# Order of the score matmuls, path of the row maxima, and order of two DMA groups in a fused attention and MLP block

## The chip, the cores and the metric

The kernel runs on one core of a Trainium2 chip. A core has five engines with a queue each: PE (TensorE, matrix products), DVE (VectorE), ACT (ScalarE), POOL (GpSimd) and SP (SyncE, which here only starts DMA transfers). Each engine works through its own queue in order, and semaphores order the queues among each other. Products go to PSUM, a small memory of banks of 512 float32 values per partition; everything else is in SBUF, with 128 partitions, or in HBM. The metric is the time of one execution on the device, in microseconds (us).

## The reference

One transformer-like block on x of 2048 tokens by 640 features, all in float32. A vector c gives six modulation vectors. Then sliding attention with 32 heads of 20 features, in which a token sees itself and the 255 tokens before it, and a channel MLP with 1536 hidden features:

```python
mod = (_silu(c) @ w_mod).reshape(c.shape[0], 6, 1, -1)
h = _layernorm(x) * (1 + ca) + sa
qkv = h @ wqkv
scores = einsum("bhqd,bhkd->bhqk", q, k) * (Dh ** -0.5)
mask = (i - j >= 0) & (i - j < 256)
p = _softmax(where(mask, scores, -1e9))
x = x + ga * ((p @ v) @ wo)
h = _layernorm(x) * (1 + cb) + sb
x = x + gb * (gelu(_layernorm(h) @ w1 + b1) @ w2 + b2)
```

## The kernel before

**Precision.** Most operands are split into a high and a low part in a reduced float32 format (`F32R`), and a product is the sum of high x high, high x low and low x high. A projected q or k thus has three rows per feature, 60 rows for the 20 features of a head.

**Stages.** First a prologue: the modulation, the first LayerNorm and the first projection units. Then the attention stage, a loop over slots `t` that is written out by hand and runs from about 50 to about 610 us of the span. Last the MLP, with the last pieces of attention's output projection mixed in.

**A slot.** The 2048 tokens are worked on in two halves of 1024 (`HALF`), the 32 heads in eight groups of four (`quad`), and the 1024 queries of a half in eight blocks of 128 (`qb`). There are 2 x 8 x 8 = 128 score slots. In slot `t` the loop issues, in this order:

- a *score batch* (`score_batch`, line 549) with two parts. The part `e` has *transposed* scores, keys on partitions, for the head group of `LAG` = 11 slots ago (`e_batch`). The part `s` has *plain* scores, queries on partitions, for the present block (`s_batch`); they are used only to find the maximum of each row.
- on DVE the mask of `e` (`e_mask`), then the sums P x V of `PVLAG` = 2 slots ago on PE (`pv_stage`, tile `o`), and the exponential of `e` on ACT (`e_exp`, tile `pt`) with two triangular selections on POOL
- on DVE the mask of `s` and the maxima of its rows (`s_max`, tile `nm`)
- the stores of q and k rows that were projected in an earlier slot (`rows_out`, line 435, on SP's queue)
- four quarters `h` = 0 to 3 of planned work (`plan`): projection matmuls (`pp`), weight loads (`w_load`, placed at the head of quarter 0), splits of weights, transposes, reads of projected rows back from HBM (`rows_in`, planned in quarter 3, up to `READ` = 7 slots before their use).

In slots whose transposed part is empty (one in eight of the first half), and in the first 11 and the last slots, the batch has one part only. `e` and `s` have one PSUM buffer each, of 4 heads x 384 columns, which is three banks.

**The halves of the array.** q and k of two heads lie at partitions 0 to 63 and 64 to 127, so a score matmul uses one half of the array's rows, and two matmuls on different halves can run at once. Of the four heads of a buffer, two belong to either half. The four heads lie at 384 columns each, so the middle bank is shared between the halves. `score_batch` sorts the matmuls of a part into six groups: `a`, `b`, `c` on the first half (`a` in the shared bank), `d`, `e`, `f` on the second (`f` in the shared bank). It puts a wait in PE's queue ahead of `f`, until the last matmul of `a` is complete. The order in which the groups are issued stands in two lists: `ONE` for batches with one part and `BOTH` for batches with two, where "0" is the transposed part, if there is one, and "1" the plain part.

**The maxima.** When the eight blocks of a head group are done, their 4 x 8 maxima per partition are negated and split into a high and a low part on DVE (`m_split`, at the end of every eighth slot, into tile `mh`). In the next slot, quarter 1, `m_rows` transposes `mh` on PE, copies the result to SBUF on ACT (tile `mt`), and starts two DMA transfers from ACT's queue, which lay the two parts into rows 60, 61 and 124, 125 of the group's q buffer. The transposed scores of that group then subtract the maximum inside the product, against rows of ones in the k buffer. They start three slots later.

`Ordered` (line 108) passes each instruction on in program order, so line 124, its helper, is the line that nearly all instructions show; they are told apart by their tiles.

Of the kernel before, what the change touches and what calls it, by code (L numbers as in the profile page):

```python
# [9 lines left out]
F32 = mybir.dt.float32  # L10
F32R = mybir.dt.float32r
U32 = mybir.dt.uint32
AF = mybir.ActivationFunctionType
ALU = mybir.AluOpType
# [3 lines left out]
P = 128  # L18
# [5 lines left out]
NQB = HALF // P  # L24
QUADS = H // 4
# [3 lines left out]
NSLOT = 4  # L29
# [24 lines left out]
X_COST = 1.7  # L54

ONE = "0a 0d 0b 0e 0c 0f".split()
BOTH = "0a 0d 1a 0b 0e 0c 1d 1c 0f 1b 1f 1e".split()

EXTRA = {
# [44 lines left out]
def f32(ap):  # L104
    return ap.bitcast(F32)
# [24 lines left out]
def block_kernel(ctx: ExitStack, tc: tile.TileContext, x, wqkv, wo, w1, b1, w2, b2, c, crow, wmod, wcol, sel, outT):  # L130
    core = tc.nc
    nc = Ordered(tc)
    matmul, transpose = nc.tensor.matmul, nc.tensor.transpose
# [20 lines left out]
    idn = const.tile([P, P], F32, name="idn")  # L154
# [45 lines left out]
    base = ctx.enter_context(tc.tile_pool(name="base", bufs=1, side="left"))  # L200
    prj = prj_ctx.enter_context(tc.tile_pool(name="prj", bufs=1, side="left"))
    att_ctx = ExitStack()
    att = att_ctx.enter_context(tc.tile_pool(name="att", bufs=1, side="right"))
# [13 lines left out]
    def aside(shape, name):  # L217

        kind = "e" if now[0] < LAG - 1 else "o" if now[0] < 2 * NQB * QUADS else "t"
        return pools[kind].tile(shape, F32, tag=kind, name=name)  # L220
# [168 lines left out]
    qb_ = [att.tile([P, 2, HALF], F32R, name=f"qbuf{i}") for i in range(NSLOT)]  # L389
# [45 lines left out]
    def rows_out():  # L435

        due = [w for w in writes if w[-1] < now[0]]
        for half, kind, j, c2, st, _ in due:
            fs, ts = slice(j * P, (j + 1) * P), slice(half * HALF + c2 * CHUNK, half * HALF + (c2 + 1) * CHUNK)
            two = f32(st) if kind == 0 else f32(st[:, 0:1]).to_broadcast([P, 2, CHUNK])  # L440
            nc.sync.dma_start(qk_scr[kind][fs, 0:2, ts], two)
            nc.sync.dma_start(qk_scr[kind][fs, 2, ts], f32(st[:, kind]))
        del writes[: len(due)]
# [105 lines left out]
    def score_batch(batches):  # L549
# [19 lines left out]
        }  # L569
        order = BOTH if len(batches) == 2 else ONE  # L570
        queue = [(int(k in "def"), mm) for n, k in order for mm in kinds.get((int(n), k), ())]
# [33 lines left out]
        nc.vector.copy_predicated(s[:, :, 2 * P : 384], masks["s"].to_broadcast([P, 4, P]), data)  # L605
        nc.vector.tensor_reduce(it["quad"]["nm"][:, :, it["key"][2]], s[:, :, max(c0, P) : 384], AX.X, ALU.max)

    mh = att.tile([P, P], F32R, name="mh")

    mh_parts = mh[:, 0:64].rearrange("p (e l r) -> p e l r", e=2, l=2)  # L610
    nc.vector.memset(f32(mh)[:, 64:P], 0.0)

    def m_split(it):
        nm, hi, lo = it["quad"]["nm"].rearrange("p (e a) q -> p e (a q)", e=2), mh_parts[:, :, 0], mh_parts[:, :, 1]
        nc.vector.tensor_scalar(hi, nm, -1.0, None, ALU.mult)
        nc.vector.scalar_tensor_tensor(lo, nm, -1.0, f32(hi), ALU.mult, ALU.subtract)

    def m_rows(it):
        half, quad, _, _ = it["key"]
        ps = aside([P, P], f"pm{half}_{quad}")  # L620
        transpose(ps, f32(mh), idn)
        mt = att.tile([64, P], F32, tag="mt", name=f"mt{half}_{quad}")
        nc.scalar.copy(mt, ps[0:64])
        for e in range(2):
            to = qb_[(half * QUADS + quad) % NSLOT][64 * e + 60 : 64 * e + 62]
            nc.scalar.dma_start(f32(to), mt[32 * e : 32 * e + 32])


    def e_parts(it):
# [21 lines left out]
    def e_mask(it, e):  # L651
        if it["mask"] == "do":

            nc.vector.copy_predicated(e[:, :, 0:P], masks["d"].to_broadcast([P, 4, P]), e[:, :, 2 * P : 384])
            return
        for col in (0, 2 * P):
            nc.vector.copy_predicated(
                e[:, :, col : col + P], masks[it["mask"]].to_broadcast([P, 4, P]), negc.to_broadcast([P, 4, P])
            )
# [134 lines left out]
    def r_steps(ch):  # L794

        ts, box = slice(ch * CHUNK, (ch + 1) * CHUNK), {}

        def load():
            pool, tag = (att, "mt") if ch < 2 else (base, "acc")
            box["rd"] = pool.tile([P, P if ch < 2 else D], F32, tag=tag, name=f"rd{ch}")[:, 0:P]  # L800
            nc.sync.dma_start(box["rd"], o_scr[:, DH, ts])

        def invert():
            nc.vector.reciprocal(box["rd"], box["rd"])
            nc.sync.dma_start(r_scr[:, ts], box["rd"])

        return load, invert
# [206 lines left out]
    for c2 in range(2):  # L1014
        for kind in range(2):
            acc = ps_0.tile([P, CHUNK], F32, tag=f"a{c2}{kind}", name=f"pp{c2}_{kind}_0")
# [104 lines left out]
    def take_aside(t, go):  # L1121

        t += AFTER.get(taken[0], 0)
        taken[0] += 1
        while t in asides:
            t += 1
        asides.add(t)
        put(t, 1, go)
        return t

    def lay_units(room):
        used, act = collections.Counter(), collections.Counter()
        for t in asides:
            used[t] += 0.5
        t, turns, where = 0, {}, []
        for i, (key, c2) in enumerate(seq):
            fast = i < FAST
            acc = (lambda i=i: pools["o"].tile([P, CHUNK], F32, tag="o", name=f"ppo{i}")) if fast and i % 2 else None
            mms, ev = unit(*key, c2, gp, acc)
            if key[0] and 2 + c2 in turns:  # L1140
                t = max(t, turns[2 + c2] + 1)
            t0, left = t, list(mms)
            pieces = []
            while left:
                have = room * (t + 1 - FAST) - sum(used[j] for j in range(FAST, t + 1))
                n = len(left) if fast else min(len(left), max(LEAST, int(have + 0.5) + EXTRA.get(t, 0)))
                if len(left) - n < 3 and n < MOST:
                    n = len(left)
                pieces.append((t, left[:n]))
                used[t] += n  # L1150
                left = left[n:]
                t += 1
            where.append((i, key, c2, pieces, ev))
            if key[1] == 2:
                used[t] += V_COST
            if not key[0] and not [1 for k, c in seq[i + 1 :] if not k[0] and c == c2]:

                at = max(t, turns[2] + 5) if c2 else t
                for kt in range(KT):
                    used[at + kt] += X_COST  # L1160
                turns[2 + c2] = at + KT + (1 if c2 else 2)
        return t, where, turns

    lo, hi = 4.0, 16.0
    for _ in range(30):
        room = (lo + hi) / 2
        lo, hi = (lo, room) if lay_units(room)[0] <= LAST else (room, hi)
    _, where, turns = lay_units(hi)
# [34 lines left out]
    for half in range(2):  # L1203
# [4 lines left out]
        for quad in range(QUADS):  # L1208
            if half or quad:
                js = range(4 * quad * DH // P, (4 * quad * DH + 4 * DH - 1) // P + 1)  # L1210
                due = 8 * (half * QUADS + quad)
                for c2 in range(2):
                    t = due + 4 * c2 - READ
                    for kind in range(2):
                        t = max([t, due - 8 * NSLOT + LAG + 8] + [over_at.get((kind, j, c2), -9) + 2 for j in js])
# [3 lines left out]
    for n, ((g, at), lo) in enumerate(zip(((2, 0), (4, 1), (3, 2), (5, None)), MODS)):  # L1219
        steps, rows = mod_steps(g, at)  # L1220
        spread(plan, [step(1, f) for f in steps], lo[0], lo[1])
        t = int(lo[1])
        for f in rows:
            t = take_aside(t, f) + 1
    for ch, when in turns.items():
# [7 lines left out]
        t = when  # L1233
        for kt in range(KT):
            t = take_aside(t, lambda gos=turn[3 * kt : 3 * kt + 3]: [go() for _, go in gos]) + 1
# [26 lines left out]
    for t, nm, go in sorted(tail, key=lambda e: e[:1]):  # L1262
        t = t if t < 128 else 128 + (t - 128) / LATE
        if nm not in ("load", "om"):
            t = max(t, TOMID)
# [19 lines left out]
    for t in range(n + LAG + PVLAG + 4):  # L1285
        now[0] = t
        si = s_items[t] if t < n else None
        u = t - LAG
        ei = e_items[u] if 0 <= u < n else None
        if t == n:  # L1290
            sco_ctx.close()
            pools["t"] = ctx.enter_context(
                tc.tile_pool(name="ps_t", bufs=1, space=PSUM, side="left", reuse_waits="tile")
            )
        turn_m = 8 <= t <= n and t % 8 == 0
        batches = []
        if ei and ei["kbs"]:
            batch, e = e_batch(ei)
            batches.append(batch)
        if si:  # L1300
            batch, *got = s_batch(si)
            batches.append(batch)
        score_batch(batches)
        if ei and ei["kbs"]:
            e_mask(ei, e)
        sums = [(*key, pv_stage(*key)) for key in pv_at.get(t, ())]
        if t not in SUMS_LAST:
            for each in sums:
                pv_copy(*each)
        if ei and ei["kbs"]:  # L1310
            e_exp(ei, e)
        if t in SUMS_LAST:
            for each in sums:
                pv_copy(*each)
        if si:
            s_max(si, *got)
            if t % NQB == NQB - 1:
                m_split(si)
        rows_out()
        for h in range(4):  # L1320
            if h == 1 and turn_m:
                m_rows(s_items[t - 1])
            for go in plan.pop((t, h), ()):
                go()
        for key in pv_at.get(t, ()):
            pv_store(*key)
# [20 lines left out]
    for ch in range(nch):  # L1347
        yhi, ylo = ([y[:, kt] for kt in range(KT)] for y in yT[ch % 2])
        ts = slice(ch * CHUNK, (ch + 1) * CHUNK)
        lo, hi = (4, 9) if ch == 0 else (4 * ch + 5, 4 * ch + 9)  # L1350
# [21 lines left out]
        for f in range(FT):  # L1372
# [7 lines left out]
            pool, tag = (ps_out, f"o{KT - 1}") if (ch, f) == (0, 1) else (ps_h, "h")  # L1380
# [68 lines left out]
```

## Time and profile before

| | us |
|---|---|
| median of three runs | 1017.7 |
| the three runs | 1014.81, 1017.7, 1019.65 |
| span of the profiled execution (its own time from first to last instruction) | 1014.6 |
| PE busy in the span | 962.9 (95%) |
| DVE busy | 576.7 (57%) |
| POOL busy | 513.2 (51%) |
| ACT busy | 443.7 (44%) |

The profiled execution's own time is known by its span; what lies around it is not recorded on the page. Matmuls are pipelined and the ends of their records are modelled, so a record is longer than the time that the matmul keeps others away, and a busy PE is not one at its peak. The time between the starts of two matmuls says more than their lengths. Idle time in the list of waits is counted per engine, and PE's weight loads (PEld) are kept apart from its matmuls (PE). A wait is put down to the instruction that came last by the records. An engine that waits costs nothing by that alone: it matters where PE, busy for 95% of the span, stands behind it.

### The profile page before, as it was taken

Reading aid. Unit: us, or ns where it says so; the run is one execution under the profiler, and the core shown is the slowest. Engines: PE = TensorE matmul, PEld = TensorE weight load, DVE = VectorE, ACT = ScalarE, POOL = GpSimd, SP = SyncE. Lnnn points to the kernel's source line nnn. Section 1 sums busy time; section 2 is a strip of 40 time slices with the busy share of each in tenths; the row PEclk is TensorE's granted clock in tenths of the full one; section 3 lists DMA queues with packets and bytes.
Section 4 is the critical chain, followed back from the end, with each engine's and each line's share of the span. In section 5 each row is a group of like instructions: output and inputs, shape, how many; then the busy total and the mean of one; then the engine's idle time right before and its main releaser. Section 6 shows DMA issues by size and latency. Waiting matters only on the chain.

```text
span 1014.6 us, 19923 instructions
## 1 busy us (share of the span) xinstructions
PE 962.9 (95%) x7712; PEld 761.1 (75%) x7712; DVE 576.7 (57%) x943; ACT 443.7 (44%) x773; POOL 513.2 (51%) x702
## 2 busy tenths in 40 slices
PE   7989999998999999999988889999999999999998
PEld 7767677666677777776666667888888888888886
DVE  5554777887777788777778753454433343333112
ACT  3732555565654455455534544434433333333212
POOL 4332646676774456455535754666455445541221
PEclk7899999999999999999978889999999999999999
DMA  8255858656588467945482124244333234124113
GB/s 297 94 199 162 278 173 267 211 157 176 170 265 245 126 202 245 285 107 161 125 245 62 45 77 130 94 153 140 120 112 87 81 117 135 48 70 154 54 40 117
DMA packets 99429, 152.89 MB, mean 151 GB/s; under 512 B 8904, under 2 KB 42312, under 8 KB 99336
## 3 DMA queue, kind: packets, MB, share of 16 engines
q1 hardware_dynamic: 89032, 142.71, 46.1%
q10 hardware_dynamic: 10304, 8.92, 2.9%
q8 instruction: 61, 1.00, 0.4%
q14 instruction: 32, 0.26, 0.1%
HBM read 99.17 MB, written 51.58 MB: 149 GB/s over the span
## 4 chain that ended last, share of the span: by engine, by line
PE 78%; DVE 11%; ACT 4%; DMA 3%; issue 2%; POOL 1%; SPq 0%; ACTq 0%; DVEq 0%; POOLq 0%
PE h L124 16%; PE out L124 16%; PE pp L124 15%; PE wo L124 7%; PE e L124 6%; PE o L124 6%; PE s L124 6%; DVE nm L124 3%; DVE e L124 3%; ACT pt L124 2%; DVE s L124 2%; PE ppo L124 2%; PE psx L124 1%; DMA o_scr<-oT 1%; PE xt L124 1%
## 5 line engine op out<-in xcount | busy, mean ns | idle before, releaser
L124 POOL TENSOR_SCALAR_AFFINE_SELECT pt<-pt 128x512 f32<-128x512 f32 x192 | 130.5, 680 | 137.3 <-ACT pt L124 123.9
L124 DVE TENSOR_REDUCE nm<-s 128x4 f32<-128x1024 f32 (+1 forms) x128 | 152.7, 1193 | 4.4
L124 POOL TENSOR_TENSOR w2lo<-w2r,w2hi 128x640 fp32r<-128x640 f32 x48 | 75.6, 1575 | 151.8 <-ACT w2hi L124 151.4
L124 ACT ACTIVATE pt<-e 128x1024 f32<-128x1024 f32 (+1 forms) x120 | 133.8, 1115 | 38.4 <-DVE e L124 34.0
L124 PE MATMUL e<-qbuf,kbuf 62*128 62x128 f32 (+2 forms) x792 | 120.7, 330 | 21.5 <-ACT pt L124 21.2
L124 PEld LDWEIGHTS e<-qbuf,kbuf 62*128 62x128 f32 x792 | 82.4, 193 | 62.9 <-ACT pt L124 39.2
L124 PE MATMUL pp<-hhi,whi 128*128 128x512 f32 x275 | 120.1, 437 | 3.9 <-ACT hhi L124 1.5
L124 DVE CAST ghi<-g 128x512 fp32r<-128x512 f32 x48 | 26.5, 553 | 166.3 <-ACT g L124 166.2
L124 PE MATMUL s<-kbuf,qbuf 60*128 60x256 f32 (+2 forms) x744 | 111.3, 304 | 9.5 <-DVE nm L124 8.2
L124 PE MATMUL pp<-hlo,whi 128*128 128x512 f32 x275 | 112.3, 408 | 0.6 <-POOL hlo L124 0.6
L124 PEld LDWEIGHTS s<-kbuf,qbuf 60*128 60x128 f32 x744 | 91.3, 189 | 27.7 <-PE e L124 8.7
L124 PE MATMUL pp<-hhi,wlo 128*128 128x512 f32 x275 | 112.0, 407 | 0.0
L124 DVE COPY_PREDICATED e<-mask_t,e 128x512 f32<-128x512 uint32 x96 | 66.6, 694 | 75.4 <-PE s L124 64.2
L124 ACT COPY oT<-o 128x128 f32<-128x128 f32 x128 | 34.0, 266 | 169.7 <-PE o L124 162.3
L124 PE MATMUL o<-pt,vbuf 128*32 128x128 f32 x2688 | 104.5, 287 | 0.7 <-ACT oT L124 0.4
L124 POOL TENSOR_TENSOR wlo<-wraw,whi 128x128 fp32r<-128x128 f32 x185 | 81.3, 470 | 34.2 <-ACT whi L124 31.8
L124 PE MATMUL out<-ghi,w2hi 128*128 128x512 f32 x240 | 96.1, 400 | 0.0
L124 PE MATMUL h<-yhi,w1hi 128*128 128x512 f32 x240 | 95.8, 399 | 0.0
L124 PE MATMUL out<-ghi,w2lo 128*128 128x512 f32 x240 | 93.9, 391 | 0.0
L124 PE MATMUL out<-glo,w2hi 128*128 128x512 f32 x240 | 93.9, 391 | 0.0
L124 PE MATMUL h<-ylo,w1hi 128*128 128x512 f32 x240 | 93.9, 391 | 0.0
L124 PE MATMUL h<-yhi,w1lo 128*128 128x512 f32 x240 | 93.8, 391 | 0.0
(166 smaller groups left out, 1842.1 us busy)
## 6 DMA issues: line engine op xcount, KB each, us to landing
w2r<-in_w SPq DMA_DIRECT2D x48, 320.0 KB
qbuf<-q_scr SPq DMA_DIRECT2D x60, 240.0 KB
wraw<-in_wqkv SPq DMA_DIRECT2D x38, 320.0 KB
kbuf<-k_scr SPq DMA_DIRECT2D x44, 240.0 KB
q_scr<-stage SPq DMA_DIRECT2D x20, 512.0 KB
k_scr<-stage SPq DMA_DIRECT2D x20, 512.0 KB
o_scr<-oT ACTq DMA_DIRECT2D x64, 128.0 KB
wm<-in_wmod SPq DMA_DIRECT2D x20, 320.0 KB
```

Source lines behind the costliest of these rows:

```text
L124: return self.tc.keep_in_program_order(op(*args, **kw))
```

## The change

Three things are changed, all in the attention stage.

1. In a batch with two parts, all groups of the transposed part are issued first, in the order `a d c e b f`, then all groups of the plain part in the same order. Before, the parts were mixed. The wait ahead of `f` stays as it is, once for each part.
2. `m_split` and its tile are gone. `m_rows` transposes the 32 columns of maxima as they are, and then splits: ACT negates into `mt` and rounds that to the high part, POOL subtracts for the low part. The two DMA transfers are issued from SP's queue; one has the high parts (rows 60 and 124), the other the low parts (rows 61 and 125). The reciprocal sums, which shared the buffer `mt`, get a buffer of their own (`rd`).
3. `rows_out` moves from ahead of the four quarters to the head of quarter 1. On SP's queue it now stands behind what quarter 0 issues, the weight loads above all, and ahead of `m_rows`.

```diff
-BOTH = "0a 0d 1a 0b 0e 0c 1d 1c 0f 1b 1f 1e".split()
+BOTH = "0a 0d 0c 0e 0b 0f 1a 1d 1c 1e 1b 1f".split()
...
-    mh = att.tile([P, P], F32R, name="mh")
-
-    mh_parts = mh[:, 0:64].rearrange("p (e l r) -> p e l r", e=2, l=2)
-    nc.vector.memset(f32(mh)[:, 64:P], 0.0)
-
-    def m_split(it):
-        nm, hi, lo = it["quad"]["nm"].rearrange("p (e a) q -> p e (a q)", e=2), mh_parts[:, :, 0], mh_parts[:, :, 1]
-        nc.vector.tensor_scalar(hi, nm, -1.0, None, ALU.mult)
-        nc.vector.scalar_tensor_tensor(lo, nm, -1.0, f32(hi), ALU.mult, ALU.subtract)
-
     def m_rows(it):
         half, quad, _, _ = it["key"]
-        ps = aside([P, P], f"pm{half}_{quad}")
-        transpose(ps, f32(mh), idn)
-        mt = att.tile([64, P], F32, tag="mt", name=f"mt{half}_{quad}")
-        nc.scalar.copy(mt, ps[0:64])
-        for e in range(2):
-            to = qb_[(half * QUADS + quad) % NSLOT][64 * e + 60 : 64 * e + 62]
-            nc.scalar.dma_start(f32(to), mt[32 * e : 32 * e + 32])
+        ps = aside([4 * NQB, P], f"pm{half}_{quad}")
+        transpose(ps, it["quad"]["nm"].rearrange("p h q -> p (h q)"), idn)
+        hi = att.tile([4 * NQB, P], F32R, tag="mhi", name=f"mhi{half}_{quad}")
+        lo = att.tile([4 * NQB, P], F32R, tag="mlo", name=f"mlo{half}_{quad}")
+        full = att.tile([4 * NQB, P], F32, tag="mt", name=f"mt{half}_{quad}")
+        nc.scalar.mul(full, ps, -1.0)
+        nc.scalar.copy(hi, full)
+        nc.gpsimd.tensor_tensor(lo, full, f32(hi), ALU.subtract)
+        for row, part in ((60, hi), (61, lo)):
+            nc.sync.dma_start(f32(qb_[(half * QUADS + quad) % NSLOT][row::64]), f32(part))
...
-            pool, tag = (att, "mt") if ch < 2 else (base, "acc")
+            pool, tag = (att, "rd") if ch < 2 else (base, "acc")
...
-            if t % NQB == NQB - 1:
-                m_split(si)
-        rows_out()
         for h in range(4):
+            if h == 1:
+                rows_out()
             if h == 1 and turn_m:
                 m_rows(s_items[t - 1])
```

## The prediction

> **What bounds the kernel now.** I read the page first: its span, and the chain that ended last.
>
> ```profile
> span 1014.6 us, 19923 instructions
> PE 78%; DVE 11%; ACT 4%; DMA 3%; issue 2%; POOL 1%; SPq 0%; ACTq 0%; DVEq 0%; POOLq 0%
> ```
>
> PE carries 78% of the chain and DVE 11%. The second question is what PE waits for, so the list of waits comes next, longest first.
>
> ```profile
> DVE e L124 <- PE s L124: 81.8, 79, 3.2
> PE e L124 <- ACT pt L124: 21.2, 25, 2.4
> PE s L124 <- DVE nm L124: 8.2, 20, 1.3
> ```
>
> Both of PE's large waits are in the attention stage, and both are loops from one slot to the next: a batch of transposed scores (`e`) waits until the exponential of the slot before has read the one buffer, and a batch of plain scores (`s`) until the maximum of the slot before has been taken. The first row shows a third thing: the mask of `e` on DVE begins when plain scores end, although it needs `e` alone.
>
> All this happens inside the double batches, so I looked at single slots in the timeline. First PE in a slot where nothing is late, then DVE and ACT in the same slot (columns: start, length, engine, operation, tiles, count).
>
> ```profile
> 322.83 0.44 PE L124 MATMUL e<-qbuf,kbuf 62*128 62x256 f32 x2
> 323.05 0.28 PE L124 MATMUL s<-kbuf,qbuf 60*128 60x256 f32 x1
> ...
> 323.17 0.54 PE L124 MATMUL e<-qbuf,kbuf 62*128 62x128 f32 x3
> 323.46 0.43 PE L124 MATMUL s<-kbuf,qbuf 60*128 60x384 f32 x4
> 323.82 0.54 PE L124 MATMUL o<-pt,vbuf 128*32 128x128 f32 x12
> ```
>
> ```profile
> 323.91 0.70 DVE L124 COPY_PREDICATED e<-mask_t,e 128x512 f32<-128x512 uint32 x1 [1.36 <-PE s L124]
> 324.51 0.69 DVE L124 COPY_PREDICATED s<-mask_t,s 128x512 f32<-128x512 uint32 x1
> 325.24 1.23 DVE L124 TENSOR_REDUCE nm<-s 128x4 f32<-128x1024 f32 x1
> ```
>
> The mixed batch of 6 + 6 matmuls takes 0.99 us from its first matmul to the first `o` (322.83 to 323.82): `e` and `s` fill each other's holes. The mask starts at 1.08, and the maxima are done at 3.64.
>
> **Part 1, the order of the batch.** The `e` matmuls of the two row halves of the array share one bank of the buffer. The program lets the second half's part of it ("f") start only when the first half's part ("a") is complete; PE's own queue stands at that wait. There is one such wait for `e` and one for `s`. Slots that have `e` alone show its price, since nothing else fills the hole.
>
> ```profile
> 593.42 0.88 PE L124 MATMUL e<-qbuf,kbuf 62*128 62x256 f32 x6
> 594.24 0.65 PE L124 MATMUL o<-pt,vcar 128*32 128x128 f32 x16
> 593.42 0.41 PEld L124 LDWEIGHTS e<-qbuf,kbuf 62*128 62x128 f32 x5 [0.19 <-ACT pt L124]
> 593.92 0.18 PEld L124 LDWEIGHTS e<-qbuf,kbuf 62*128 62x128 f32 x1
> 594.41 0.70 DVE L124 COPY_PREDICATED e<-mask_t,e 128x512 f32<-128x512 uint32 x1 [2.02 <-PE e L124]
> ```
>
> Five weight loads lie in the first 0.41 us. The sixth, that of "f", comes only 0.50 us after the first, and the whole single batch takes 0.82 (593.42 to 594.24). In the new order all six `e` matmuls come first, so "f" of `e` stands before the first `s`, and the queue stands too: the first `s` load cannot pass. Then the `s` half repeats the same pattern with its own wait. A new double batch thus takes 0.50 + 0.82 = 1.32 us, against 0.99: **+0.33 us**. In the old order seven groups, some of them of the other batch, stand between each "a" and its "f"; in the new one four, all of its own batch.
>
> I found 109 double batches between 104.95 and 569. Of these 21 have nine `e` matmuls and are longer already; one of them:
>
> ```profile
> 314.91 0.44 PE L124 MATMUL e<-qbuf,kbuf 62*128 62x128 f32 x4
> 316.03 0.42 PE L124 MATMUL o<-pt,vbuf 128*32 128x128 f32 x8
> ```
>
> It takes 1.12 now (314.91 to 316.03) and 1.32 then, +0.20. The gross cost is 88 x 0.33 + 21 x 0.20 = 29.0 + 4.2 = **33 us**. Its bounds: 0 if the wait did not bind, and 109 x (2 x 0.82 - 0.99) = 71 if the two batches did not overlap at all. I take the value from the load row, which is the same mechanism at the same clock.
>
> Against it stand two gains. First, the wait of `s` on the maxima. The list's 8.2 us counts only what left PE wholly idle; the first `s` matmul itself is late in 52 of the 109 batches. First and last of them:
>
> ```profile
> 104.95 0.44 PE L124 MATMUL e<-qbuf,kbuf 62*128 62x256 f32 x2
> 105.69 0.35 PE L124 MATMUL s<-kbuf,qbuf 60*128 60x256 f32 x1 [0.30 <-DVE nm L124]
> 557.79 0.45 PE L124 MATMUL e<-qbuf,kbuf 62*128 62x256 f32 x2
> 558.30 0.38 PE L124 MATMUL s<-kbuf,qbuf 60*128 60x256 f32 x1
> ```
>
> They are 0.74 and 0.51 behind the first `e`, where 0.22 is normal (322.83 to 323.05). Summed over the 52, the lateness is 15.0 us. In the new order `s` starts at 0.50 anyway, 0.28 later; the mask of `e` starts at 0.99 (593.42 to 594.41) in place of 1.08 or more, as it no longer waits for `s`, so the maxima end 0.1 earlier; and the slot is up to 0.33 longer. Lateness under 0.7 then goes, and none is over 0.67. I take **14 us** of the 15.
>
> Second, the wait of `e` on the exponential: 21.2 us at 25 places in the list. A head that waits swallows up to 0.33 of the longer batch ahead of it. Taking for each head the smaller of its wait and what its batch grows by, short waits included, I get 7; the mask that starts 0.1 earlier adds 0.1 at some 20 longer ones. I take **8 us**; the bounds are 0 and 21.2. What is late next in those slots is the exponential still, after batches with nine matmuls above all, with two masks and a longer exponential.
>
> **Part 2, the maxima transposed whole.** Removed from DVE: 16 times the two splits. Moved from ACT's queue to SP's: 32 stores.
>
> ```profile
> L124 DVE TENSOR_SCALAR mh<-nm x16: 181/181/1284, 91.0 to 569.1; 128x32 fp32r<-128x32 f32 x16
> L124 DVE SCALAR_TENSOR_TENSOR mh<-nm,mh x16: 191/646/661, 91.2 to 569.8; 128x32 fp32r<-128x32 f32 x16
> L124 ACTq DMA_DIRECT2D qbuf<-mt x32: 620/622/1240, 97.5 to 574.5; - x32
> L124 ACT COPY mt<-pm x16: 246/252/261, 97.2 to 573.6; 64x128 f32<-64x128 f32 x16
> PEld e L124 <- ACT mt L124: 3.3, 9, 0.4
> ```
>
> DVE loses 0.8 us in one slot of eight, where the next mask waits for PE anyway; ACT loses 2 x 0.62 of issue and gains a second copy of about 0.25; POOL gains one small subtraction, 0.25 to 0.5. None is on PE. What matters is when the rows land: `e` of that head group first reads them three slots on. The path gets longer, since POOL's subtraction stands behind the two selections of its slot, and SP behind the stores of projected rows. A slot with all of that in it, at 185.14:
>
> ```profile
> 189.79 1.34 POOL L124 TENSOR_SCALAR_AFFINE_SELECT pt<-pt 128x512 f32<-128x512 f32 x2
> 189.87 0.90 SPq L124 DMA_DIRECT2D q_scr<-stage  x2
> 190.83 0.82 SPq L124 DMA_DIRECT2D wraw<-in_wqkv  x1
> 198.15 0.45 PE L124 MATMUL e<-qbuf,kbuf 62*128 62x256 f32 x2
> q_scr<-stage SPq DMA_DIRECT2D x20, 512.0 KB
> q_scr<-stage SPq DMA_DIRECT2D x20, 256.0 KB
> wraw<-in_wqkv SPq DMA_DIRECT2D x38, 320.0 KB
> ```
>
> The selections end at 191.13; with the subtraction 191.6; two issues of 0.62 bring it to 192.9. Ahead in the same queue lie at most 512 + 256 + 320 KB, 3.6 us at the 300 GB/s that the core reaches when it is full (row below), so the rows land by about 195 to 196. The first reader starts at 198.15, and three longer batches later still. I cost this part at **0**, covered by 2 to 3 us; without that cover each microsecond of lateness is a microsecond of PE, in up to 15 head groups. The other bound is a gain of 3.3 us: so long, 9 times, a weight load of `e` came behind ACT's copy of the maxima; but each of these is under 0.4, and a copy stays on ACT. The tile for the sums' reciprocals gets a buffer of its own, which costs nothing: it takes a possible wait away.
>
> **Part 3, projected rows behind the weight loads.** On SP the weight load of a slot, and whatever else stands in its first quarter, now goes ahead of up to 3 stores of 256 and 512 KB. The store's reader is planned at least two slots behind the projection unit; its staging tile is one of four; and the maxima's stores of part 2 stand behind both. Above, SP had the load 0.9 us behind the stores, so a load comes about 1 us sooner. A store may come later by the load's wait for a free buffer. None of PE's waits of any size names a load of weights or a staging tile, so I take **0**, with 2 us either way.
>
> **The sum.** 33 - 14 - 8 + 0 + 0 = **+11 us**. The profiled execution shows a span of 1014.6; the median of the runs, 1017.7, is 3.1 above it and their spread is 4.8. I add the 11 to the median and forecast **1029 us**, 1.1% slower. The bound for "no change" is 0.5%, 5.1 us, about what a measurement of this kernel can tell.
>
> **Rivals.**
>
> *Faster: the wait costs nothing.* If "a" were complete when the queue reaches "f", the double batch would stay at 0.99 and only the gains stay: 14 of the first kind, and 0.1 us of earlier mask at the 25 long heads of the second, 2.5 us; 1017.7 - 16.5 = 1001. This decides from the point where the batch grows by less than (14 + 8) / 109 = 0.20 us. Against it: the sixth weight load at 593.92, with nothing before it in the queue but the wait. Chance 0.07.
>
> *No change: the weight loads pass the wait.* If PE loaded the weights of the first `s` matmuls while the queue stands at "f", the second half would start some 0.1 us sooner, and its own "f" as well: the batch would grow by about 0.23 (0.10 for one with nine), gross 22, and the sum would be 0, 1018 us. Against it: in the single batch the load of "f" itself was not done ahead, although the array had idle rows from 593.83 on. Chance 0.09. The Trainium skill ("TensorE: Matmul & The Clock Gate", "Architectural detail") says that PE's queue is a partial reorder window that pulls weight loads ahead of matmuls in flight. By that rule this case would be the likely one; the load row here differs from it where a wait stands between. The Trainium skill ("TensorEngine Tiling (Array Packing)", "Gotcha 1: PSUM Pressure") also says that different row tiles must not access the same bank at once and that software has to see to it, so the wait cannot be left out; that agrees with the hole in these rows.
>
> *Slower still: the maxima land late.* If loads from the first quarter of the slot and stores together hold SP's queue for 3 us more than I allowed, `e` stands once per head group. Only some 5 of the 15 groups have stores in that slot; 2 us each gives 10 on top of the forecast, 1039 us. Chance 0.10.
>
> *Slower still: the clock.* The granted clock halves after a thin stretch of PE:
>
> ```profile
> 511.18:514.59 3.41, 0.98 (x20) 0.65 (x13) 2.92 (x4) 2.16 (x3) 1.54 (x1) 1.00 0.96 278
> 514.59:518.00 3.41, 2.61 (x36) 1.97 (x33) 3.09 (x5) 0.78 (x2) 0.00 (x0) 0.50 1.03 306
> 415.60:419.00 3.40, 2.35 (x31) 1.45 (x23) 3.24 (x4) 1.61 (x2) 3.40 (x6) 1.00 1.05 302
> ```
>
> A stretch with 0.98 us of matmuls in 3.41 was followed by half clock; one with 2.35 (415.60) was not. The new holes take 0.33 of a slot of some 3.8 us, 9%, so 2.35 would become about 2.1, still far from 0.98. Two more halved stretches of 10 us would cost 5 us each: 1039. The same account may also take one of the existing ones away. Chance 0.07. The Trainium skill ("TensorE: Matmul & The Clock Gate", "What's actually happening") has the gate set by how busy PE was over a window of about 3.4 us, which these rows agree with.
>
> **How the numbers follow.** The forecast's own mechanism has 0.67, with its terms uncertain by some 7 us: 1022 to 1036. The first rival has 0.07 near 1001, the second 0.09 near 1018, the last two together 0.17 near 1039. The range 1016 to 1042 leaves out the first rival and the far end of the last two. Faster by over 0.5%: 0.08, the first rival and a little of the second. Within 0.5%: 0.14, most of the second and the forecast's low end. Slower: 0.78.
>
> **What the profile after would show.** Six `e` matmuls in a row, the first `s` 0.50 us behind them, and 1.32 us from the first `e` to the first `o`. The mask of `e` 0.99 after the first `e`, waiting for PE `e` and no longer for PE `s`. PE's wait of `s` on the maxima close to nothing, its wait of `e` on the exponential near 13 us in place of 21. No split on DVE, no store of maxima on ACT's queue, and no new wait of `e` on a transfer. The stretch from 104.95 to the last `e` longer by 11, and what follows it as long as before. The prediction is wrong if the double batch is under 1.2 us, if `e` waits for the maxima's stores, or if the half-clock stretches change in number.

## The result, and the profile after

The changed kernel takes 1034.28 us (median; 1031.83 to 1035.09) against 1018.23 for the kernel before on the same chip: a ratio of 1.0153, with an interval of 1.0127 to 1.0179. The forecast was 1029, slower, and the sign and the mechanism hold. The loss is 5 us larger than forecast; which terms of the sum missed is told below.

The page's span and its chain, of the kernel after:

```profile
span 1032.5 us, 20057 instructions
...
PE 86%; DVE 5%; ACT 4%; POOL 3%; issue 2%; DMA 1%; SPq 0%; ACTq 0%; POOLq 0%; DVEq 0%
```

PE's share of the chain rose from 78% to 86%, DVE's fell from 11% to 5%: the two loops over DVE and ACT became looser while PE itself became longer. The list of waits shows the same (us in total, times, longest):

```profile
DVE e L124 <- PE e L124: 72.1, 55, 4.2
DVE e L124 <- PE s L124: 45.8, 39, 2.3
PE e L124 <- ACT pt L124: 11.1, 21, 1.3
PE e L124 <- DMA qbuf<-mlo: 5.4, 1, 5.4
PE s L124 <- DVE nm L124: 1.8, 3, 0.9
```

PE's wait of `e` on the exponential went from 21.2 to 11.1 and that of `s` on the maxima from 8.2 to 1.8; the mask of `e` now waits mostly for `e`. The 39 masks that the second row still puts down to `s` start as early as the others, 0.99 us (median) behind the first `e` and 0.44 behind the first of several `s`, so that row does not show a wait for all of `s`. One row is new and was not forecast: a wait of 5.4 us for a store of maxima.

Three batches of the kernel after in the timeline, each with its first `e`, first `s` and first `o` (start, length, engine, operation, tiles, count):

```profile
306.75 0.82 PE L124 MATMUL e<-qbuf,kbuf 62*128 62x256 f32 x6
307.29 0.85 PE L124 MATMUL s<-kbuf,qbuf 60*128 60x256 f32 x6
308.07 0.64 PE L124 MATMUL o<-pt,vbuf 128*32 128x128 f32 x16
...
294.57 0.88 PE L124 MATMUL e<-qbuf,kbuf 62*128 62x256 f32 x6
295.22 0.85 PE L124 MATMUL s<-kbuf,qbuf 60*128 60x256 f32 x6
296.01 0.86 PE L124 MATMUL o<-pt,vbuf 128*32 128x128 f32 x24
...
314.75 0.89 PE L124 MATMUL e<-qbuf,kbuf 62*128 62x256 f32 x6
315.52 0.85 PE L124 MATMUL s<-kbuf,qbuf 60*128 60x256 f32 x6
316.31 0.75 PE L124 MATMUL o<-pt,vbuf 128*32 128x128 f32 x20
```

Each has six `e` in a row and then six `s`, but they take 1.32, 1.44 and 1.56 us, and the first `s` comes 0.54, 0.65 and 0.77 behind the first `e`. Forecast was 1.32 and 0.50 for all. The weight loads of "f" and of the first two `s`, and DVE's work, in the middle one:

```profile
295.07 0.18 PEld L124 LDWEIGHTS e<-qbuf,kbuf 62*128 62x128 f32 x1
295.19 0.22 PEld L124 LDWEIGHTS s<-kbuf,qbuf 60*128 60x128 f32 x2
```

```profile
295.56 0.69 DVE L124 COPY_PREDICATED e<-mask_t,e 128x512 f32<-128x512 uint32 x1 [1.52 <-PE e L124]
296.16 0.69 DVE L124 COPY_PREDICATED s<-mask_t,s 128x512 f32<-128x512 uint32 x1
296.88 1.23 DVE L124 TENSOR_REDUCE nm<-s 128x4 f32<-128x1024 f32 x1
```

"f" is loaded 0.50 us behind the first `e` (295.07 to 294.57), as forecast, and no load of `s` passes it. The mask of `e` starts at 0.99. Both steps stand.

**Where the time went.** The stretch from the first `e` of the first double batch to the first `e` behind the last one grew by 19.9 us (104.95 to 568.79 before, 103.58 to 587.34 after):

```profile
568.79 0.88 PE L124 MATMUL e<-qbuf,kbuf 62*128 62x256 f32 x6
```

```profile
103.58 0.89 PE L124 MATMUL e<-qbuf,kbuf 62*128 62x256 f32 x6
...
587.34 0.89 PE L124 MATMUL e<-qbuf,kbuf 62*128 62x256 f32 x6
```

What follows it is as long as before (1032.5 - 587.3 = 445.2, and 1014.6 - 568.8 = 445.8), and 1.4 us went ahead of it. The profiled execution of the kernel before is the fastest of its four, so the two spans differ by 17.9 and not by 16.05. From the starts of the matmuls in this stretch, summed:

| us | forecast | measured |
|---|---|---|
| 109 double batches, first `e` to first `o` | +33 - 14 = +19 | 129.4 to 156.2, +26.8 |
| PE stands ahead of a batch, those with one part included | -8 | 35.1 to 27.8, -7.3 |
| of that, one late store of maxima | 0 | +5.4 |
| sum | +11 | +19.5 |

Of the 7.3 us, 4.8 are ahead of the double batches and 2.5 ahead of those with one part.

### The profile page after: what moved, and what is told of

It reads as the page before. It is cut to its first block, busy times and chain, and to the rows that moved or that the text cites. A ratio compares the mean times of both kernels' runs of the same rounds, so it can differ in the third digit from the quotient of the medians.

```text
span 1032.5 us, 20057 instructions
## 1 busy us (share of the span) xinstructions
PE 991.4 (96%) x7712; PEld 779.1 (75%) x7712; DVE 568.5 (55%) x910; ACT 448.8 (43%) x789; POOL 520.1 (50%) x718
## 4 chain that ended last, share of the span: by engine, by line
PE 86%; DVE 5%; ACT 4%; POOL 3%; issue 2%; DMA 1%; SPq 0%; ACTq 0%; POOLq 0%; DVEq 0%
PE pp L124 18%; PE h L124 16%; PE out L124 15%; PE e L124 9%; PE o L124 8%; PE s L124 7%; PE wo L124 6%; ACT pt L124 3%; DVE e L124 2%; PE ppo L124 2%; PE psx L124 1%; PE yt L124 1%; PE xt L124 1%; POOL y L124 1%; PE pv L124 1%
## 5 line engine op out<-in xcount | busy, mean ns | idle before, releaser
L124 ACT ACTIVATE pt<-e 128x1024 f32<-128x1024 f32 (+1 forms) x120 | 133.9, 1116 | 27.3 <-DVE e L124 26.1
L124 PEld LDWEIGHTS e<-qbuf,kbuf 62*128 62x128 f32 x792 | 77.1, 193 | 64.6 <-ACT pt L124 25.9
L124 PE MATMUL e<-qbuf,kbuf 62*128 62x128 f32 (+2 forms) x792 | 108.7, 327 | 16.7 <-ACT pt L124 11.1
L124 PE MATMUL s<-kbuf,qbuf 60*128 60x256 f32 (+2 forms) x744 | 108.6, 316 | 2.4 <-DVE nm L124 1.8
L124 PEld LDWEIGHTS s<-kbuf,qbuf 60*128 60x128 f32 x744 | 77.1, 190 | 20.7 <-PE pp L124 4.8
```

The lines of the kernel that those rows point to most:

```text
L124: return self.tc.keep_in_program_order(op(*args, **kw))
```

## The experiments

**The order alone.** The kernel before with the one line changed:

```diff
-BOTH = "0a 0d 1a 0b 0e 0c 1d 1c 0f 1b 1f 1e".split()
+BOTH = "0a 0d 0c 0e 0b 0f 1a 1d 1c 1e 1b 1f".split()
```

> The kernel before with the new order of the batch alone; the maxima and the stores stay as they were. Theory: nearly all of the loss comes from here. In the changed kernel the double batches grew from 129.4 to 156.2 us in all, and the waits of e at the head of a batch, without the one for the maxima's store, fell by some 12: I expect +14 us (+11 to +18), the first s 0.54, 0.66 or 0.77 behind the first e, and PE's wait of e on a transfer gone. Rival: half or more of the loss comes from the path of the maxima and from SP's queue, which block PE in ways that the list of waits shows only in part: then this run is +3 to +9.

Measured: 1031.02 us against 1015.72, a ratio of 1.0155 (1.0117 to 1.0194). The order carries the whole loss. Its double batches take 153.9 us in sum, 24.5 more than before.

**The maxima alone.** The kernel before with the second part of the change:

```diff
-        transpose(ps, f32(mh), idn)
...
+        transpose(ps, it["quad"]["nm"].rearrange("p h q -> p (h q)"), idn)
...
+        nc.gpsimd.tensor_tensor(lo, full, f32(hi), ALU.subtract)
```

> The kernel before with the new path of the maxima alone; the order of the batch and the place of the stores stay. Theory: one head group, at the slot where loads of the output projection stand ahead on SP's queue, finds its rows late, and that costs up to 5 us; the other groups have cover: 0 to +6 us. Rival: +7 to +14, with e waiting for the maxima's stores in several groups.

Measured: a ratio of 0.9984 (0.9964 to 1.0003), 1.6 us less. The interval just takes in no change. PE's wait of `e` on a store of maxima is there too, 4.9 us in 2 places, but the wait of `e` on the exponential is 15.4 in place of 21.2. Some of that may be the same time under another name, as a wait for two things is put down to the later one; this was not separated.

**The stores alone.** The kernel before with the third part:

```diff
-        rows_out()
         for h in range(4):
+            if h == 1:
+                rows_out()
```

> The kernel before with the stores of projected rows in quarter 1 alone. Theory: nothing, within 2 us either way. Rival: +3 us or more, since a weight load that waits for its buffer holds the stores, and their staging tiles, back.

Measured: a ratio of 1.0027 (1.0008 to 1.0046), 2.7 us more. Its double batches are no longer than before (128.7 in sum), PE's wait of `s` on the maxima is as it was (8.1), and that of `e` on the exponential rose from 21.2 to 23.6. What made the exponential later wasn't followed up. Added up by their ratios, the three parts give 1.55 - 0.16 + 0.27 = 1.66%, and together 1.53% were measured (1.27 to 1.79).

**The hole filled.** The kernel after with an order in which two groups of `s` stand between "0a" and "0f":

```diff
-BOTH = "0a 0d 0c 0e 0b 0f 1a 1d 1c 1e 1b 1f".split()
+BOTH = "0a 0d 0c 0e 0b 1a 1d 0f 1c 1e 1b 1f".split()
```

> The changed kernel, but the first two groups of s are issued ahead of f of e, so that PE's queue has work while a is not yet complete. Theory: the hole at f is what costs; with it filled the first s comes at 0.35 to 0.45 and the batch takes 1.05 to 1.2 in place of 1.35 to 1.55, and at least 12 us of the 16 come back: -2 to +6 us against the kernel before. Rival: what costs is that s comes after e at all, or the path of the maxima; then less than 6 us come back: +10 to +16.

Measured: a ratio of 1.0013 (0.9994 to 1.0032). Two groups moved into the hole give 14 us back, and everything else of the change is still there. A batch of this kernel:

```profile
288.78 0.56 PE L124 MATMUL e<-qbuf,kbuf 62*128 62x256 f32 x4
289.12 0.39 PE L124 MATMUL s<-kbuf,qbuf 60*128 60x384 f32 x1
...
289.99 0.54 PE L124 MATMUL o<-pt,vbuf 128*32 128x128 f32 x12
```

It takes 1.21 us, a little over the 1.05 to 1.2 expected, and the first `s` stands 0.34 behind the first `e`, within 0.02 of it in 74 of the 109 batches: the spread from 0.54 to 0.77 is gone with the hole. The double batches take 137.5 us in sum, 18.7 less than in the kernel after and still 8.1 more than before. The late store is there as well, with a wait of 5.6.

**Waits that are met.** That spread was the open question. In the kernel's instruction list, the waits that a matmul cannot carry itself stand in PE's queue as instructions of their own: the one ahead of "f" in some batches, one for the maxima, and in slots where a new block of keys comes in one or two for the transfers that brought it. Sorted by how many of them stand between the first `e` and the first `s`, the batches of the kernel after with six `e` fall into steps (the three batches above have 1, 2 and 3):

| waits | batches | first `s`, median | to the first `o`, median |
|---|---|---|---|
| 0 | 2 | 0.46 | 1.29 |
| 1 | 30 | 0.54 | 1.35 |
| 2 | 41 | 0.66 | 1.44 |
| 3 | 15 | 0.77 | 1.55 |

Either each wait costs about 0.11 us, met or not, or these are lateness of what is waited for. So two waits were added ahead of the first `s`, both for work that was done long before:

```diff
+        old = [i for i in (masked.get(now[0] - 1), picked.get(now[0] - 2)) if i is not None]
...
+            while n == 1 and old:
+                tc.add_manual_dep(nc.tensor.nop().ins, old.pop().name, in_order, reason="done long ago")
```

> The kernel after, with up to two more waits in PE's queue directly ahead of the first s of a batch, both met long before: one for the mask of the slot before on DVE, one for the selection two slots back on POOL. The program has 501 wait instructions on PE in place of 422, 79 more. Theory (a wait instruction costs PE about 0.12 us where nothing else stands ready in its queue, met or not: in the kernel after, the first s comes 0.54 us behind the first e with none in that place, 0.66 with one, 0.77 with two): the first s about 0.1 later at each of them, 79 x 0.12 = 9.5 us longer than the kernel after, near 1.025 of the kernel before. Rival (a wait that is met costs nothing, and the spread from 0.54 to 0.77 is the lateness of what is waited for): as the kernel after, 1.015.

Measured: 1036.45 us, a ratio of 1.0181 (1.016 to 1.0202), 2 to 3 us above the kernel after and not 9.5; the intervals of the two overlap, so the times alone don't tell the two theories apart. The trace does. The same two slots as the first and third above:

```profile
308.35 0.82 PE L124 MATMUL e<-qbuf,kbuf 62*128 62x256 f32 x6
309.00 0.85 PE L124 MATMUL s<-kbuf,qbuf 60*128 60x256 f32 x6
...
316.57 0.88 PE L124 MATMUL e<-qbuf,kbuf 62*128 62x256 f32 x6
317.44 0.85 PE L124 MATMUL s<-kbuf,qbuf 60*128 60x256 f32 x6
```

The first `s` is at 0.65 where it was at 0.54, and at 0.87 where it was at 0.77: one step up each, for a wait that was met. Over the 79 batches with one wait more the first `s` moved by 0.095 us on average; over the other 30 by nothing (-0.004). The step is shown. What failed is its price: the batches grew by 6.1 us in sum, the stretch by 4.0 (483.8 to 487.8). PE's stands ahead of a batch took up 1.4 of the difference (27.8 to 26.4). The rest is open, and the clock may have a part in it: the stretch has 27.3 us at half clock in the kernel after and 20.5 in this one, an estimated 3.4 us at most in favour of this one. The batches at full clock in both grew by 6.8.

**The same waits in the old order.** They were added to the kernel before, with the same lines.

> The kernel before, with the same 80 met waits ahead of the first s of a batch (414 wait instructions on PE in place of 334). There the first s stands behind only two matmul groups of e, and matmuls of the two score halves follow mixed. Theory (a wait instruction is hidden as long as matmuls that are already loaded are still streaming behind it): 0 to 2 us longer, 1.000 to 1.002 of the kernel before. Rival (each costs its 0.12 us wherever it stands): 80 x 0.12 = 9.6 us, 1.009.

Measured: a ratio of 1.0020 (1.0000 to 1.0041), at the upper end of "hidden". The double batches grew by 2.5 us in sum for 80 waits, where the new order's grew by 6.1 for 79. But this profile is of the slowest of its ten runs, with 34.1 us of the stretch at half clock where the kernel before has 17.1; the batches at full clock in both grew by 1.4 only. In the mixed order most of it is covered, if not all.

**The wait for the maxima moved ahead.** In the kernel after, PE was to wait for the maxima ahead of the third group of `e`:

```diff
+            if len(batches) == 2 and half and not done:
+                done = 1
+            elif done == 1 and not half:
+                done = 2
+                tc.add_manual_dep(nc.tensor.nop().ins, taken_[0].name, in_order, reason="maxima of the slot before")
```

> The kernel after, with the wait for the maxima of the slot before moved from directly ahead of the first s to ahead of the third group of e (0c), where matmuls of 0a and 0d still run; no wait is added (422 on PE in both). Theory (the place of the wait instruction is what costs): the first s at 0.54 in place of 0.66 behind the first e in most batches, 0.08 to 0.12 us in some 80 batches, so 6 to 9 us off the kernel after: 1.006 to 1.009 of the kernel before. Where the maxima are late, e now waits with s, which gives up to 2 us back. Rival (the wait is free, s is late because of its semaphore): no gain, 1.015, or a loss of some us from the waits that now hold e too.

Measured: a ratio of 1.0169 (1.0150 to 1.0189), no gain. But the instruction list shows that this was no test of the theory: the matmul of group "0c" carries the new wait itself, and the old one still stands ahead of the first `s`. The steps of the first `s` are unchanged (0.54, 0.66 and 0.77 for 1, 2 and 3). All it says is that a wait carried by a matmul, in a place where others stream, does not show here. Whether the waits in that place can be done without wasn't tried.

**An order that beats both.** The kernel before, with the first `s` behind four groups of `e` and groups of `s` in the hole:

```diff
-BOTH = "0a 0d 1a 0b 0e 0c 1d 1c 0f 1b 1f 1e".split()
+BOTH = "0a 0d 0b 0e 1a 1d 0c 0f 1c 1b 1f 1e".split()
```

First together with the new maxima, transposed one quarter earlier, and the stores where they were before:

> The kernel before with the maxima of part 2, their transposition at the head of the slot's first quarter, the stores of projected rows where they were, and the batch order 0a 0d 0b 0e 1a 1d 0c 0f 1c 1b 1f 1e: two groups of s between the last two pairs of e, so that the hole between 0a and 0f is filled, and the first s still behind four groups of e. Theory (the kernel after loses by the hole alone; an order in which other work stands in the hole keeps the old length of the batch and takes part of the 15 us of late s away): 0 to 5 us faster than before, 0.995 to 1.000. Rival (any order with s later than third keeps a hole): 3 to 10 us slower, 1.003 to 1.010.

Measured: 1011.18 us, a ratio of 0.9944 (0.9927 to 0.9962). Then the order alone:

> The kernel before with one line changed, the batch order 0a 0d 0b 0e 1a 1d 0c 0f 1c 1b 1f 1e. Theory (most of the 5.9 us by which the version with this order and the new maxima beat the kernel before comes from the order: the double batches are 124.8 us in sum there against 129.4): 3 to 5 us faster than before, 0.995 to 0.997. Rival (the new maxima alone bring it, as 1.6 us were measured for them alone, and their earlier place the rest): 0 to 1 us, 0.999 to 1.000.

Measured: 1005.83 us, a ratio of 0.9894 (0.9869 to 0.9918), 9 us faster than the kernel before by the medians, 11 by the ratio, and the fastest here; more than expected. A batch of it:

```profile
289.16 0.45 PE L124 MATMUL e<-qbuf,kbuf 62*128 62x256 f32 x3
289.45 0.33 PE L124 MATMUL s<-kbuf,qbuf 60*128 60x256 f32 x1
...
290.16 0.70 DVE L124 COPY_PREDICATED e<-mask_t,e 128x512 f32<-128x512 uint32 x1 [1.53 <-PE e L124]
290.20 0.64 PE L124 MATMUL o<-pt,vbuf 128*32 128x128 f32 x16
```

It takes 1.04 us, and its mask starts at 1.00 and waits for `e`. This is what the change's own order set out from, without its hole. The double batches are 4.5 us shorter in sum than before (124.9), the stands ahead of a batch 3.5 (31.6); the stretch is only 5.7 shorter (458.2), with 20.5 us at half clock in place of 17.1. Another 2.7 lie ahead of the stretch in these two executions, where the program is the same, so 5 to 6 us is what the profile accounts for.

The new maxima, transposed one quarter earlier, thus cost about 5 us in this order. Two things in the version with both can make them cost that. One is in its list of waits:

```profile
PE pm L124 <- ACT oT L124: 5.4, 14, 0.4
```

PE stands ahead of the transposition (`pm`) until ACT has copied the sums `o`, with which it shares its PSUM buffer, in 14 of the 16 groups; with the order alone this is 0.8 in 2. The other is a store that comes late, as in each kernel that has the new maxima on SP's queue:

```profile
495.21 0.66 SPq L124 DMA_DIRECT2D ob<-o_scr  x1
...
500.93 0.45 POOL L124 TENSOR_TENSOR mlo<-mt,mhi 32x128 fp32r<-32x128 f32 x1
...
502.91 0.56 SPq L124 DMA_DIRECT2D r<-r_scr  x1
503.57 0.55 SPq L124 DMA_DIRECT2D xb<-in_x  x1
504.17 0.91 SPq L124 DMA_DIRECT2D kbuf<-k_scr  x2
505.17 0.59 SPq L124 DMA_DIRECT2D qbuf<-mhi  x1
505.81 0.56 SPq L124 DMA_DIRECT2D qbuf<-mlo  x1
...
511.20 0.80 PE L124 MATMUL e<-qbuf,kbuf 62*128 62x256 f32 x4 [5.79 <-DMA qbuf<-mlo]
```

SP issues nothing from 495.87 to 502.91: the load of `r` waits in its queue until POOL has last read the tile that had the same buffer (`ga_b`, at 502.89), and the stores of maxima, whose last data POOL had ready at 501.38, stand behind it until 505.17.

**The stores on ACT's queue.** The kernel after, and then the version with both, with this line changed:

```diff
-            nc.sync.dma_start(f32(qb_[(half * QUADS + quad) % NSLOT][row::64]), f32(part))
+            nc.scalar.dma_start(f32(qb_[(half * QUADS + quad) % NSLOT][row::64]), f32(part))
```

> The kernel after, with the two stores of maxima of a group issued from ACT's queue, where those of the kernel before were, in place of SP's. In the kernel after one group stood 4.7 us in SP's queue (520.60 to 522.85, behind loads of r, xb and kbuf) and the e that needs it waited 5.4 us. Theory (that one transfer costs its wait, less what the e would have waited anyway): the wait of e on the store of mlo gone, 3 to 5 us off the kernel after, 1.010 to 1.012 of the kernel before. Rivals: e waits for its exponential as long (0 to 1 us off, 1.015); or ACT, which now issues for 2 x 0.62 us and waits for POOL's subtraction first, holds the exponentials up, 16 times 0.5 us (8 us longer, 1.023).

> The version with both (order 0a 0d 0b 0e 1a 1d 0c 0f 1c 1b 1f 1e, maxima transposed whole at the head of the first quarter), with the maxima stores issued from ACT's queue. There one group came 5.8 us late on SP's queue; on ACT's it can be 2.9 us late at most, by when POOL's subtraction ends. Theory: 3 to 5 us faster than that version, 0.989 to 0.992 of the kernel before. Rival (ACT's issues, 32 x 0.62 us, push exponentials): as that version or slower, 0.994 or above.

Measured: 1.0257 (1.0232 to 1.0281) for the first, some 10 us slower than the kernel after, and 0.9978 (0.9959 to 0.9997) for the second, 3 to 4 us slower than the version with both. Both are worse than SP's queue. The theory fell, and the rival that ACT holds the rest up holds. ACT's waits on the maxima in the first:

```profile
ACT oT L124 <- DMA qbuf<-mlo: 13.0, 4, 3.9
ACT oT L124 <- POOL mlo L124: 3.4, 1, 3.4
ACT ot L124 <- POOL mlo L124: 3.1, 1, 3.1
PE e L124 <- DMA qbuf<-mlo: 3.1, 2, 1.6
```

ACT stands at the low part's store until POOL's subtraction, behind POOL's selections, is done, and with it ACT's next copies. The stretch grew by 7.0 us (483.8 to 490.8). Another 3.7 lie ahead of it, but they are no price of the stores: they arise between 56 and 68 us, where this execution has a stretch at half clock (55.9 to 66.1) that the kernel after has not, and the first of these stores is issued at 100.07. The six executions of this kernel were granted a clock of 0.967 to 0.972, the four of the kernel after 0.972 to 0.978, so some of the 10 us may be clock, and whether the moved stores bring that about is not shown. So the price of the one late store could not be had back this way, and what it is worth stays open, in the kernel after as in the version with both, where PE's wait ahead of the transposition is a second candidate for the 5 us.

## Why the prediction was right, and where it missed

- *The hole between "a" and "f".* Right. The load of "f" comes at 0.50, no load of `s` goes past it, and the order alone explains the whole loss, as filling the hole explains its return. The rival "the wait costs nothing" is out, and so is "the weight loads pass the wait". The Trainium skill ("TensorE: Matmul & The Clock Gate", "Architectural detail") says that PE's queue can pull weight loads ahead of matmuls in flight; past a wait, this case's rows show none pulled (295.07 and 295.19).
- *The gross cost of 33 us.* Mis-sized. The step that failed is "0.50 + 0.82 = 1.32 us" for all batches: it took the first `s` to follow "f" at once. By the table a batch with six `e` takes 1.29, 1.35, 1.44 or 1.55, which is 2 x -0.03 + 30 x 0.03 + 41 x 0.12 + 15 x 0.23 = 9 us more. What took the time are the wait instructions ahead of the first `s`. PE has 334 of them in the kernel before, 417 with the order alone and 422 after, so most of the new ones came with the order; single batches, from which the 1.32 was put together, don't have them between two parts. It is their place that counts: the kernel with the hole filled has 440. The miss in the table is 7.8 and not 9: the batches before were also longer than the prediction's own numbers make them, by 3.8 us (88 x 0.99 + 21 x 1.12 + 15.0 = 125.6, where 129.4 was measured), and smaller misses add to the 9.
- *The gain of 14 on late `s`.* Nearly right: of the 15.0 us of lateness, 2.4 remain in 13 batches, by the same table.
- *The gain of 8 on the stands ahead of `e`.* The wait on the exponential went to 11.1 where 13 was forecast, and all stands to 27.8 from 35.1. Without the late store's wait they would have gone down by 12.7, by an estimate that takes it as lost in full; 2.5 of that is ahead of batches with one part, which the forecast did not count. That this term came out close to the forecast is luck: longer batches swallow more, and a store gave 5.4 back.
- *Part 2 at 0, "covered by 2 to 3 us".* Wrong for one group of 16, right in the sum when made alone (-1.6). The step that failed is "ahead in the same queue lie at most 512 + 256 + 320 KB": that was read from one slot at 185 us, and later slots have loads of another stage in the same queue. In the kernel after:

```profile
512.52 0.67 SPq L124 DMA_DIRECT2D ob<-o_scr  x1
520.60 0.56 SPq L124 DMA_DIRECT2D r<-r_scr  x1
...
523.55 0.55 SPq L124 DMA_DIRECT2D qbuf<-mlo  x1
...
528.90 0.98 PE L124 MATMUL e<-qbuf,kbuf 62*128 62x256 f32 x6 [5.41 <-DMA qbuf<-mlo]
```

```profile
517.00:521.00 4.00, 2.93 (x41) 2.06 (x40) 2.87 (x4) 2.10 (x5) 3.20 (x4) 1.00 0.02 4
521.00:525.00 4.00, 2.26 (x39) 1.78 (x39) 2.90 (x5) 1.84 (x5) 2.30 (x3) 1.00 0.60 192
525.00:529.00 4.00, 0.10 (x2) 0.13 (x2) 1.50 (x2) 1.17 (x3) 0.51 (x1) 0.73 1.05 264
```

```profile
519.02 1.55 POOL L124 TENSOR_TENSOR wor<-wor,ga_b 128x640 f32<-128x640 f32 x1
520.54 0.45 POOL L124 TENSOR_TENSOR mlo<-mt,mhi 32x128 fp32r<-32x128 f32 x1
```

  SP stands from 513.19 to 520.60 at the load of `r`, with the DMA engines idle at its end (the last columns of the stretches are granted clock, DMA share and GB/s: 0.02 of them busy from 517 to 521). By the kernel's buffers and the times it waits until POOL has last read `ga_b`, whose buffer `r` takes over (519.02 + 1.55 = 520.57). POOL's subtraction for the maxima stands behind the same multiplication and is done at 520.99. Its store then comes 2.6 us later, behind the loads that had queued up, which start all at once and keep the DMA engines full, and the rows land at about 528.9. The rival "the maxima land late" had the right place but the wrong cause: it was no load of the first quarter and no store of projected rows, and it struck one group and not five. A wait of `e` for the maxima's stores was one of the prediction's own signs of being wrong; it came, and that the sum stayed within 5 us of the forecast in spite of it and of the 9 us above is in part luck.
- *Part 3 at 0, "with 2 us either way".* Made alone it costs 2.7 (0.8 to 4.6), at the edge.
- *The clock.* The rows of granted clock on the page, of before and of after, show the dip at the same place and of about the same depth. Between 500 and 640 us the trace has four stretches at half clock in either kernel, 34.1 us in all before and 37.5 after, so they did not change in number. Of these, 17.1 and 27.3 us lie in the stretch that grew by 19.9, which is worth an estimated 5 us there at most. It is not what made the batches longer: the 103 that are at full clock in both kernels grew by 0.24 us each.

```profile
PEclk7899999999999999999978889999999999999999
```

```profile
PEclk7899999999999999999977989999999999999999
```

## What to carry to other kernels

In a queue that works in order, ask for each wait what already issued work still streams behind it: the price of a dependence is the hole it leaves, and moving two groups of other work into the hole gave 14 us back here, and an order chosen for it, without the other parts, ran 9 us faster than the kernel before. When batches are joined from pieces that were measured singly, look for the instructions that stand between the pieces alone. Before a transfer is moved to another queue, walk that queue over the whole stage, for the loads of other stages that may stand and wait there, and not over one slot.

## What the runs showed of the hardware

- A wait instruction in PE's queue takes about 0.11 us right behind another wait that has let PE's work run out, also when it was met long before (0.54, 0.66, 0.77 and 0.87 us to the first `s` for 1, 2, 3 and 4 of them). In an order with work still streaming it hardly shows: 80 more of them moved the first `s` of the batches by 1.0 us in sum in the old order, 79 by 7.4 in the new one.
- A transfer that waits in SP's queue stops the transfers behind it, also those whose data is ready, and the backlog then runs together: in the version with both, the low parts were ready at 501.38, were stored at 505.81 and let `e` start at 511.20; in the kernel after, 7.4 us of standing was followed by 4 us with the DMA engines full (1.05 from 525 to 529).
